# Moving half of one batch's exponentials from the SP queue to the ScalarE queue

## The chip, the cores and the metric

One Trainium2 chip; the kernel runs on one of its cores. The metric is the device time of one execution in microseconds (us). The engines are TensorE (PE: matrix products, with PEld for its weight loads), VectorE (DVE), ScalarE (ACT), GpSimd (POOL) and SyncE (SP). A transfer (DMA) is issued by an engine's queue, here SP's or ScalarE's (SPq and ACTq in the rows), and moved by DMA engines; each engine works through its own list of instructions in order, and they wait for each other with semaphores.

## What is computed

The reference is an attention of tokens against a small state, in both directions, and then a feed-forward network over both results. For each of 8 batches and 8 heads, with 512 tokens `x` and 32 state rows of 64 numbers:

```
scores  = scale * x @ state.T      a  = softmax(scores)     xread = a @ state
scores2 = scale * state @ x.T      a2 = softmax(scores2)    sread = a2 @ x
x   = concat(xread, sread) over tokens, heads side by side: 4352 rows of 512
h   = x @ w_in                                   (512 x 2048)
out = (h * clip(h + 3, 0, 6) / 6) @ w_out        (2048 x 512)
```

All of it is in float32.

## The kernel before

**Tiles and stages.** The work goes batch by batch. The feed-forward part of a batch is cut into 16 steps, one for each 128 columns of the hidden layer; step numbers run on over all batches, 0 to 143. In step n, `first(n)` forms the hidden values of 128 columns by 512 tokens in a PSUM bank `ps_h` (six matmuls, line 858). ScalarE makes `relu(h + 3)` from it (line 908), DVE takes the minimum with 6 and multiplies by h (line 910). The result `g` is split in two halves for PE: a cast on ScalarE (line 246, `g_hi`) and a subtraction on DVE (line 247, `g_lo`). Two steps later `second(n)` multiplies it with `w_out` into four PSUM accumulators `acc0` to `acc3` (twelve matmuls, also line 858, three for each accumulator). `ps_h` has two banks, so `first(n + 2)` waits until lines 908 and 910 of step n have read theirs. The product of the state with `w_in` (called W', lines 462, 246 and 247, in the banks `ps_s`) stands in for `xread @ w_in`, so `first` multiplies the weights `a` directly with W'.

**Batches 0 and 1 at the start.** The first two batches are interleaved with the loading of the weights: steps 0 to 3 are batch 0, 4 to 11 batch 1, 12 to 23 batch 0, 24 to 31 batch 1, then batches 2 to 7 follow. At the end of step 23 the accumulators of batch 0 are added to a partial result by four additions on DVE (line 947), one for each accumulator; `second(24)` may write an accumulator of the same name only after its addition has read it.

**The state's own attention.** For `sread`, the exponentials of `scores2` of batch b (line 718, on ScalarE) come in two groups g of 128 rows, one tile `tmp` each. To be used as PE weights they have to be turned. From batch 1 on, `weights_moved` does that in two parts: DVE transposes each 32 x 32 block in place (line 766 for batch 1, into the tile `blocks`), and then 16 transfers for each group set the blocks in their places in the tile `e2T` (line 773, 16 KB each, from SBUF to SBUF). `tokens_read(1)` then multiplies `e2T` with x (line 815, 64 matmuls, the first group's before the second's). It rides in one PE operation with the scores of batch 2: a transpose of batch 0's result (line 833), the 16 score matmuls (line 462), and line 815. In the plan this operation stands right behind `first(27)`. Batches 2 to 7 do the same with line 787 and one tile for both groups.

**What sets the order.** Every operation is given to a planner (`Plan`) with an engine (T, V, S or Q for PE, DVE, ScalarE and SP's transfers), a cost, a rank, and what it reads and writes. `Plan.order` steps through time: on each engine it looks at the operations that could start, takes those that could start within 0.3 us of the soonest, and of them the one of lowest rank, and by number where ranks are equal. Results count as visible 0.12 us after an operation of DVE or ScalarE and 0.25 us after one of PE. For SP's transfers it counts at most eight in flight:

```
        flying = [0.0] * 8
                    if e == "Q":
                        t = max(t, min(flying))
                    (c for c in can if c[0] <= soon + (0.8 if c[1] <= 0.0 else 0.3)),
                    key=lambda c: c[1:],
```

The order that comes out is written into the engines' lists; on the chip the engines follow it and the semaphores. The moves of batch 1 are told with rank `MOVED` = 22. In batches 0 and 1 the ranks of lines 908 and 910 and of the split (lines 246 and 247) are the step number; the additions of line 947 after step 23 have rank 25, and W' for the steps from 28 on has 25.4. In the program every transfer, of either queue, uses one of eight completion counters, taken in turn in the order of the plan, and waits before it is issued until the transfer that used that counter last has landed.

Other lines that are spoken of: 352 (cast of a piece of `w_out`), 962 (store of a batch's result), 382 (load of a batch's state), 969 (the last two stores, one from each queue).

Of the kernel before, what the change touches and what calls it, by code (L numbers as in the profile page):

```python
# [149 lines left out]
def tile_state_attention_then_hardswish_ffn(  # L150
# [8 lines left out]
    nc = tc.nc  # L159
# [65 lines left out]
    def V(cost, rank, do, reads=(), writes=(), after=()):  # L225
        return plan.add("V", cost, rank, do, reads, writes, after)

    def S_(cost, rank, do, reads=(), writes=(), after=()):
        return plan.add("S", cost, rank, do, reads, writes, after)

    def Q(rank, size, do, reads=(), writes=(), after=()):
        return plan.add("Q", 0.45, rank, do, reads, writes, after, size)

    def get(key, make):

        if key[:2] not in made:
            made[key[:2]] = make()
        return made[key[:2]]
# [277 lines left out]
    def tmp(key):  # L516

        return get(key, lambda: att.tile([P, S], F32, name="tmp", bufs=10))
# [218 lines left out]
    def e2T_key(b, g, *part):  # L737
        return ("tmp", ("e2T", b, g), *part) if b < TURNED else ("raw", ("e2T", b), *part)

    def e2T(b, g):  # L740

        return tmp(e2T_key(b, g)) if b < TURNED else made[e2T_key(b, g)][:, g]
# [16 lines left out]
    def weights_moved(b, rank, after=()):  # L759


        quarter = lambda k: slice(k * NS, (k + 1) * NS)
        if b < TURNED:
            for g in range(NG):
                blocks_key = ("tmp", ("blocks", b, g))
                V(0.62, rank, lambda g=g, key=blocks_key: nc.vector.transpose(
                    tmp(key), tmp(("tmp", ("e2", b, g)))), [("tmp", ("e2", b, g))], [blocks_key], after)
                for c in range(P // NS):
                    for q in range(NQ):
                        def move(c=c, q=q, g=g, key=blocks_key):  # L770
                            src = tmp(key)[quarter(q)].rearrange("p (j c n) -> p j c n", j=J, n=NS)
                            dst = e2T(b, g)[quarter(c)].rearrange("p (j q n) -> p j q n", j=J, n=NS)
                            nc.sync.dma_start(dst[:, :, q], src[:, :, c])  # L773
                        Q(rank, 16.384, move, [blocks_key], [e2T_key(b, g, c, q)])
            return
        blocks_key = ("raw", ("blocks", b))
        made_of = lambda key: get(key, lambda: stage.tile([P, NG, S], F32, name="raw"))
        for g in range(NG):
            V(0.62, rank, lambda g=g: nc.vector.transpose(
                made_of(blocks_key)[:, g], tmp(("tmp", ("e2", b, g)))),  # L780
                [("tmp", ("e2", b, g))], [(*blocks_key, g)])
        for c in range(P // NS):
            for q in range(NQ):
                def move(c=c, q=q):
                    src = made_of(blocks_key)[quarter(q)].rearrange("p g (j c n) -> p (g j) c n", j=J, n=NS)
                    dst = made_of(e2T_key(b, 0))[quarter(c)].rearrange("p g (j q n) -> p (g j) q n", j=J, n=NS)
                    nc.sync.dma_start(dst[:, :, q], src[:, :, c])  # L787
                Q(rank, 32.768, move, [(*blocks_key, g) for g in range(NG)], [e2T_key(b, 0, c, q)])
# [290 lines left out]
    def begin(b, s0, shift=0):  # L1079

        spots = [s0 + p + (shift if p else 0) for p in PLAN]
        rank, after = lambda k: spots[k] + 0.45, lambda k: [first_of[spots[k]]]
        at(spots[4] + 1, attention, b, rank, after)
        at(spots[7] + 1, lambda: weights_moved(b, rank(7)))
# [10 lines left out]
    for b, s0 in (0, 4), (1, 8):  # L1095

        def late(b=b, s0=s0):
# [4 lines left out]
            else:  # L1102
                load_x(1, AGAIN, (), True)
        at(LATE_TOLD[b], late)
    at(MOVED + 1, lambda: weights_moved(1, MOVED, [first_of[MOVED]]))
    fetch(2, 28, 20)
    for b in range(2, B):
# [20 lines left out]
    for n in range(len(steps)):  # L1128
        tell(n)
        b, i, _, _ = steps[n]  # L1130
        k, c = n // FPC, i // FPC
# [56 lines left out]
```

## Time and profile before

| what | value |
|---|---|
| time before, median of 3 runs | 659.69 us (659.68 to 659.81) |
| the profiled execution's own time | 660.08 us |
| its span, first to last instruction | 658.2 us |
| granted TensorE clock, mean | 0.999 |
| PE busy | 647.7 us (98%) |
| DVE busy | 420.4 us (64%) |
| ScalarE busy | 312.1 us (47%) |
| hardware-queue transfers from SP (q1) | 130704 packets, 45.37 MB |
| hardware-queue transfers from ScalarE (q10) | 144 packets, 0.26 MB |

The span is the time between the first and the last instruction in the profile; the device time has 1.88 us around it. Busy times are sums over an engine's instructions. Line numbers are those of the kernel before. In rows, "us" after a start is the time that a piece took, "xN" the number of instructions merged in it, and a bracket at the end is the idle time of the engine before it and what ended that.

### The profile page before, as it was taken

How to read it: one execution, taken by the hardware profiler on the slowest of the kernel's cores; microseconds unless marked ns; L12 is line 12 of the kernel's file. 1: busy time of each engine (PE TensorE's matmuls, PEld its weight loads, DVE VectorE, ACT ScalarE, POOL GpSimd, SP SyncE). 2: the span in 40 equal slices, each digit the busy share in tenths (PEclk: the TensorE clock that was granted, in tenths of full speed). 3: DMA queues.
4: the chain of work that ended last, by engine and by line, in shares of the span. 5: the costliest groups of instructions: out<-in, count | busy, mean ns of one | idle time of the engine just before them, and what ended most of it. 6: DMA issues, size and time to landing. Idle time of an engine off the chain costs nothing.

```text
span 658.2 us, 9905 instructions
## 1 busy us (share of the span) xinstructions
PE 647.7 (98%) x3934; PEld 502.1 (76%) x3934; DVE 420.4 (64%) x697; ACT 312.1 (47%) x522; POOL 1.0 (0%) x7
## 2 busy tenths in 40 slices
PE   7999999999999999999999999999999999999997
PEld 7447777777777877787877877787778788788896
DVE  4999999977756845954577356934595353443552
ACT  5889686643524543533444343534344343333542
POOL 0000000000000000000000000000000000000000
PEclk9999999999999999999999999999999999999999
DMA  8904742415163043323050504041131001000101
GB/s 266 318 1 160 196 150 106 98 27 138 19 144 58 15 75 85 66 32 65 17 116 14 83 1 121 13 64 32 64 66 28 5 1 65 0 1 1 64 1 33
DMA packets 130895, 46.26 MB, mean 70 GB/s; under 512 B 119201, under 2 KB 121249, under 8 KB 130721
## 3 DMA queue, kind: packets, MB, share of 16 engines
q1 hardware_dynamic: 130704, 45.37, 27.9%
q8 instruction: 31, 0.51, 0.3%
q10 hardware_dynamic: 144, 0.26, 0.1%
q14 instruction: 16, 0.12, 0.1%
HBM read 33.03 MB, written 8.91 MB: 64 GB/s over the span
## 4 chain that ended last, share of the span: by engine, by line
PE 89%; SPq 6%; DMA 2%; DVE 1%; issue 1%; ACT 0%; DVEq 0%; ACTq 0%
PE acc L858 51%; PE ps_h L858 27%; PE ps_s L462 4%; SPq L773 2%; PE acc L927 2%; SPq L787 2%; PE ps_h L462 2%; SPq L449 1%; PE ps_h L887 1%; PE ps_h L815 1%; DMA ot<-in_x_dram 1%; DMA tmp<-tmp 1%; PE ps_s L620 1%; DMA st_raw<-in_state_dram 0%; DMA raw<-in_x_dram 0%
## 5 line engine op out<-in xcount | busy, mean ns | idle before, releaser
L858 PE MATMUL acc<-w_out_hi,g_hi 128*128 128x512 f32 x528 | 208.9, 396 | 0.0
L858 PE MATMUL acc<-w_out_lo,g_hi 128*128 128x512 f32 x528 | 205.9, 390 | 0.0
L858 PE MATMUL acc<-w_out_hi,g_lo 128*128 128x512 f32 x528 | 205.7, 390 | 0.1
L908 ACT ACTIVATE g<-ps_h,three 128x512 f32<-128x512 f32 (+1 forms) x144 | 95.7, 664 | 211.3 <-PE ps_h L858 210.4
L910 DVE SCALAR_TENSOR_TENSOR g<-g,ps_h 128x512 f32<-128x512 f32 (+1 forms) x144 | 94.6, 657 | 134.6 <-ACT g L908 133.3
L858 PEld LDWEIGHTS acc<-w_out_hi,g_hi 128*128 128x128 f32 x528 | 99.1, 188 | 34.0 <-issue 11.3
L246 ACT CAST g_hi<-g 128x512 fp32r<-128x512 f32 (+1 forms) x140 | 83.2, 596 | 81.6 <-DVE g L910 81.1
L247 DVE TENSOR_TENSOR g_lo<-g,g_hi 128x512 fp32r<-128x512 f32 (+1 forms) x140 | 92.0, 658 | 46.0 <-ACT g_hi L246 44.2
L858 PEld LDWEIGHTS acc<-w_out_hi,g_lo 128*128 128x128 f32 x528 | 99.1, 188 | 21.5 <-DVE g_lo L247 0.6
L858 PEld LDWEIGHTS acc<-w_out_lo,g_hi 128*128 128x128 f32 x528 | 99.2, 188 | 19.1
L858 PE MATMUL ps_h<-aT_hi,wp_hi 128*128 128x512 f32 (+1 forms) x248 | 90.6, 365 | 0.0
L858 PE MATMUL ps_h<-aT_hi,wp_lo 128*128 128x512 f32 (+1 forms) x248 | 89.8, 362 | 0.0
L858 PE MATMUL ps_h<-aT_lo,wp_hi 128*128 128x512 f32 (+1 forms) x248 | 89.7, 362 | 0.0
L858 PEld LDWEIGHTS ps_h<-aT_hi,wp_hi 128*128 128x128 f32 x248 | 46.8, 189 | 8.5 <-DVE g L910 0.5
L858 PEld LDWEIGHTS ps_h<-aT_lo,wp_hi 128*128 128x128 f32 x248 | 46.8, 189 | 8.2 <-issue 0.5
L858 PEld LDWEIGHTS ps_h<-aT_hi,wp_lo 128*128 128x128 f32 x248 | 46.8, 189 | 7.2
L858 PE MATMUL ps_h<-aT_hi,wp 128*128 128x512 f32 x128 | 44.6, 389 | 0.0
L858 PEld LDWEIGHTS ps_h<-aT_hi,wp 128*128 128x128 f32 x128 | 24.0, 188 | 5.0
L858 PE MATMUL ps_h<-aT_lo,wp 128*128 128x512 f32 x64 | 24.9, 389 | 0.0
L462 PE MATMUL ps_s<-w_in,stT 64*32 64x512 f32 (+1 forms) x368 | 22.9, 555 | 0.0
L546 DVE STREAM_TRANSPOSE tmp<-raw 128x512 f32<-128x512 f32 x24 | 16.4, 698 | 7.1 <-DMA raw<-in_x_dram 7.1
L247 DVE TENSOR_TENSOR wp_lo<-ps_s,wp_hi 128x512 fp32r<-128x512 f32 (+1 forms) x34 | 19.7, 618 | 0.0
(123 smaller groups left out, 504.7 us busy)
## 6 DMA issues: line engine op xcount, KB each, us to landing
out_dram<-ot SPq DMA_DIRECT2D x8, 1024.0 KB, 4.4
early<-in_moe_w_in_dram SPq DMA_DIRECT2D x7, 1024.0 KB, 6.7
xb<-in_x_dram SPq DMA_DIRECT2D x28, 256.0 KB, 4.3
raw<-in_x_dram SPq DMA_DIRECT2D x96, 64.0 KB, 2.1
early<-in_moe_w_out_dram SPq DMA_DIRECT2D x4, 1024.0 KB, 5.8
raw<-in_moe_w_out_dram SPq DMA_DIRECT2D x7, 512.0 KB, 5.3
raw<-raw SPq DMA_DIRECT2D x96, 32.0 KB, 1.9
early<-in_moe_w_in_dram SPq DMA_DIRECT2D x2, 512.0 KB, 5.9
```

The costliest lines, as they stand in the source:

```text
L246: S_(cost, rank, lambda: nc.scalar.copy(hi(), src()), reads, [writes[0]])
L247: V(cost, rank, lambda: nc.vector.tensor_tensor(lo(), src(), hi().bitcast(F32), op=ALU.subtract), [*reads, writes[0]], [writes[1]])
L449: nc.sync.dma_start(t[rows, i].rearrange("t (a c) -> t a c", c=NS), x[b, 4 * g + 2 * i + u, :, k * NS : (k + 1) * NS].rearrange("(a t) c - ...
L462: nc.tensor.matmul(out[u][cols, :], made["stT", b][rows, cols], moving(q)[rows], start=True, stop=True,)
L546: V(0.7, rank, lambda q=q, key=key: nc.vector.transpose(xT(b, q), made[key][:, q % 2]), [(*key, q % 2, u, k) for u in range(2) for k in ra ...
L620: nc.tensor.matmul(out[:, j, q], xT(b, q)[:, js], apart[:, q], start=True, stop=True,)
L773: nc.sync.dma_start(dst[:, :, q], src[:, :, c])
L787: nc.sync.dma_start(dst[:, :, q], src[:, :, c])
L858: nc.tensor.matmul(ps, l, r, start=start and k == 0, stop=stop and k == n - 1)
L908: S_(cost + 0.05, rank, lambda: nc.scalar.activation(g(), bank(ps)[:, :width], AF.Relu, bias=three), [ps], [g_key])
L910: V(cost, rank, lambda: nc.vector.scalar_tensor_tensor(g(), g(), 6.0, bank(ps)[:, :width], op0=ALU.min, op1=ALU.mult), [ps], [g_key])
L927: nc.tensor.matmul(bank(acc), made["g_hi", n][:, js], plain_out[i][1](), start=opens, stop=closes)
```

## The change

In `weights_moved`, for batch 1 alone, the 16 transfers of the second group (g = 1) are issued by ScalarE's queue, and are told to the planner as ScalarE operations of 0.5 us with the rank 22 + 2.6 = 24.6. The first group's 16 stay with SP, as transfers of rank 22.

```diff
                 for c in range(P // NS):
                     for q in range(NQ):
-                        def move(c=c, q=q, g=g, key=blocks_key):
+                        def move(c=c, q=q, g=g, key=blocks_key, queue=(nc.sync, nc.scalar)[g]):
                             src = tmp(key)[quarter(q)].rearrange("p (j c n) -> p j c n", j=J, n=NS)
                             dst = e2T(b, g)[quarter(c)].rearrange("p (j q n) -> p j q n", j=J, n=NS)
-                            nc.sync.dma_start(dst[:, :, q], src[:, :, c])
-                        Q(rank, 16.384, move, [blocks_key], [e2T_key(b, g, c, q)])
+                            queue.dma_start(dst[:, :, q], src[:, :, c])
+                        if g:
+                            S_(0.5, rank + 2.6, move, [blocks_key], [e2T_key(b, g, c, q)])
+                        else:
+                            Q(rank, 16.384, move, [blocks_key], [e2T_key(b, g, c, q)])
```

## Rows read from the trace of the kernel before

**Rows 1.** The page's first part: busy time of each engine over the span.
```profile
PE 647.7 (98%) x3934; PEld 502.1 (76%) x3934; DVE 420.4 (64%) x697; ACT 312.1 (47%) x522; POOL 1.0 (0%) x7
```

**Rows 2.** Timeline of SP's queue, 129 to 151 us: start, time taken, line.
```profile
129.25 21.59 SPq L773 DMA_DIRECT2D tmp<-tmp  x32
150.94 0.54 SPq L962 DMA_DIRECT2D out_dram<-ot  x1
```

**Rows 3.** Line 773 by itself: durations in ns (minimum, median, maximum).
```profile
L773 SPq DMA_DIRECT2D tmp<-tmp x32: 586/599/988, 129.3 to 150.2; - x32
```

**Rows 4.** Timeline of PE at `tokens_read` of batch 1, from line 833 on.
```profile
149.80 0.27 PE L833 MATMUL ps_h<-ident,tmp 128*128 128x128 f32 x1
...
152.21 0.61 PE L815 MATMUL ps_h<-xb,tmp 128*32 128x64 f32 x26 [0.37 <-DMA tmp<-tmp]
152.74 0.50 PE L858 MATMUL acc<-w_out_hi,g_hi 128*128 128x512 f32 x1
```

**Rows 5.** Timeline of PE at the same operation for batch 2.
```profile
206.56 0.27 PE L833 MATMUL ps_h<-ident,tmp 128*128 128x128 f32 x1
...
208.81 0.50 PE L858 MATMUL acc<-w_out_hi,g_hi 128*128 128x512 f32 x1
```

**Rows 6.** Line 969, the last two stores: durations in ns and starts.
```profile
L969 SPq DMA_DIRECT2D out_dram<-ot x1: 615/615/615, 653.6 to 653.6; - x1
L969 ACTq DMA_DIRECT2D out_dram<-ot x1: 659/659/659, 654.2 to 654.2; - x1
```

**Rows 7.** Timeline of DVE, 129 to 149 us.
```profile
129.81 0.71 DVE L766 STREAM_TRANSPOSE tmp<-tmp 128x512 f32<-128x512 f32 x1
...
141.35 0.69 DVE L910 SCALAR_TENSOR_TENSOR g<-g,ps_h 128x512 f32<-128x512 f32 x1
...
143.09 0.68 DVE L247 TENSOR_TENSOR g_lo<-g,g_hi 128x512 fp32r<-128x512 f32 x1
143.69 1.88 DVE L947 SCALAR_TENSOR_TENSOR ot<-acc,ot 128x512 f32<-128x512 f32 x3
145.49 1.28 DVE L247 TENSOR_TENSOR wp_lo<-ps_s,wp_hi 128x512 fp32r<-128x512 f32 x2
...
148.07 0.69 DVE L247 TENSOR_TENSOR g_lo<-g,g_hi 128x512 fp32r<-128x512 f32 x1 [0.69 <-ACT g_hi L246]
```

**Rows 8.** Chain of waits, 129 to 139 us: SP's fourth, seventh, eleventh issue; a landing.
```profile
131.79 0.60 SPq L773
...
133.71 0.60 SPq L773
...
136.30 0.60 SPq L773
...
138.23 1.85 DMA tmp<-tmp
```

**Rows 9.** Line 908 from 132.4 to 132.6 us: ScalarE's queue reads step 23's semaphore.
```profile
L908 ACTq EVENT_SEMAPHORE  x1: 17/17/17, 132.4 to 132.4; - x1
```

**Rows 10.** Timeline of ScalarE, 133 to 148 us: steps 23 to 26.
```profile
133.55 0.68 ACT L908 ACTIVATE g<-ps_h,three 128x512 f32<-128x512 f32 x1
135.60 0.67 ACT L352 CAST w_out_hi<-raw 128x512 fp32r<-128x512 f32 x1 [1.38 <-DVE raw L327]
...
136.84 0.69 ACT L908 ACTIVATE g<-ps_h,three 128x512 f32<-128x512 f32 x1
138.82 0.62 ACT L246 CAST g_hi<-g 128x512 fp32r<-128x512 f32 x1 [1.30 <-DVE g L910]
140.63 0.69 ACT L908 ACTIVATE g<-ps_h,three 128x512 f32<-128x512 f32 x1 [1.19 <-PE ps_h L858]
...
142.13 0.62 ACT L246 CAST g_hi<-g 128x512 fp32r<-128x512 f32 x1
...
147.42 0.62 ACT L246 CAST g_hi<-g 128x512 fp32r<-128x512 f32 x1 [0.76 <-DVE g L910]
```

**Rows 11.** Timeline of PE: step 24's first matmul into the fourth accumulator.
```profile
147.75 0.39 PE L858 MATMUL acc<-w_out_hi,g_hi 128*128 128x512 f32 x1
```

## Prediction

> **What bounds the kernel now.** The page's first part comes first: PE is busy 647.7 us, 98% of the span, and the other engines far less [rows 1]. So only what lets PE wait, or ends a wait, counts. The change touches one place, the 32 transfers of line 773, so I read the timelines of SP, PE, ScalarE and DVE around them. SP issues all 32 in one stretch of 21.59 us from 129.25, one every 0.645 us [rows 2], each 599 ns long [rows 3]. Their reader is `tokens_read` of batch 1, the matmuls of line 815, and PE shows a wait of 0.37 us for the last of them, up to 152.21 [rows 4]. That understates it: from line 833 to the next line 858 the stretch takes 152.74 - 149.80 = 2.94 us here, and the same work in batch 2, whose transfers are in time, takes 208.81 - 206.56 = 2.25 [rows 4, 5]. So late transfers cost **0.69 us**, and no other wait of PE hangs on them. That is the whole prize: 0.1% of the time.
>
> **What is removed.** SP loses 16 issues, 16 x 0.645 = 10.3 us, and is done at about 139.6. Behind them on SP stand the store of batch 0 [rows 2] and then the load of batch 3's state; they go earlier, and no engine waits for either: nothing gained. If the second group lands before 151.0, the 0.69 us go, and the next thing late there is nothing that PE shows.
>
> **What is added.** ScalarE gets 16 issues. Its one issue in this trace, the last store, takes 659 ns against 615 for SP's store of the same size [rows 6]. Scaled, 599 x 659 / 615 = 0.64, with SP's gap of 0.045 it is 0.69 us each, 11.0 in all. Bounds: 0.645 (as SP) and 0.70 (the store's own, with the gap). I take 0.69, from the same engine.
>
> **Where they stand in ScalarE's order.** The planner decides this by rank. The moves have 24.6, steps up to 24 rank lower and go first, step 25 and its W' halves (25.4) rank higher and go last. Worked by hand from the planner's costs (0.5 a move, about 0.65 an activation or copy, its 0.3 us of choice): one move before the scaling of the last weight piece, three behind step 23's activation, one behind its cast, two behind step 24's activation, and the remaining **nine behind step 24's cast, ahead of step 25's activation**. On DVE the same working puts step 25's line 910 between the second and the third of the four line 947 additions, which empty the accumulators of batch 0, and its line 247 between the third and the fourth. Before, both stood ahead of the last three additions [rows 7].
>
> **When they run.** In the program each transfer takes one of eight completion counters in turn, over both queues, and is issued when the transfer eight places before it in the plan has landed (the planner's `flying` has eight entries too). Interleaved with SP's sixteen, the second move waits for SP's fourth, the fourth for its seventh, the fifth for its eleventh. SP's times are 131.79, 133.71 and 136.30, and one lands 1.85 us later [rows 8]: 133.64, 135.56, 138.15. ScalarE's queue works ahead of its engine: step 23's semaphore was read at 132.4, a microsecond before that activation ran [rows 9, 10]. So an issue can lie beside the activation before it, but not beside a wait. Step by step:
> - First move at 130.55, when the second transposition is done (129.81 + 0.71, [rows 7]); three from 133.65 to 136.25. The cast of line 352, at 135.60 before [rows 10], slips 0.65, and step 23's cast with it: both have slack.
> - Fifth move at 138.15, so step 24's activation is at 138.87 instead of 136.84 [rows 10]. Two moves; its cast at 140.35.
> - Nine moves from 140.3: 9 x 0.69 = 6.2. **Step 25's activation starts at 146.5 instead of 140.63** [rows 10].
> - Behind it, by start to start: 0.72 to DVE's 910, 0.78 to the cast (140.63, 141.35, 142.13), 0.65 to the 247 (147.42, 148.07), 0.60 to the last 947 (143.09, 143.69), 0.69 until it is done [rows 7, 10]: 3.44, or 149.95.
> - PE's step 24 writes the fourth accumulator at 147.75 [rows 11]. It may not until the last 947 has read it: a stall of **2.2 us**. The third is free earlier, by the same sum without the cast, the 247 and one 947, and its wait lies inside this.
> - Behind the last 947 DVE has the two W' subtractions and step 26's 910, 1.28 + 0.69 [rows 7]: 151.9, and with that the bank is free that line 833 writes; PE gets there at 149.80 + 2.2 = 152.0. No second stall. The last move lands at 147.7, in time.
>
> Sum: + 2.2 - 0.69 = **+1.5 us**. The profiled execution is 660.08, its span 658.2 and 1.88 around it; it would be 661.6. It lies 0.39 above the median of 659.69, and on that I put 661.2. About 0.2%, 1.3 us, is what a measurement of this kernel tells from no change, so 661.2 is just beyond it.
>
> The nearest rows for two queues issuing at once are the last two stores: SP's runs from 653.6 for 0.615, ScalarE's starts at 654.2 [rows 6]. They hardly overlap, so the trace leaves open whether one queue's issue holds up the other's. Bounds: nothing, and a full issue (0.645) per move while SP still issues; I take nothing, since the later store is longer by only 0.044.
>
> **Rivals.**
> *ScalarE is early enough* (not slower). If the counters never bind and a move costs 0.645 as on SP, the fifth move goes at 136.25, step 24's activation and cast stay at 136.84 and 138.82, and nine moves end at 144.7. The point that decides is 147.75 - 3.44 = 144.3 for step 25's activation with no stall, and 145.0 with a stall equal to the prize. At 144.7 the stall is 0.4: 659.69 + 0.4 - 0.69 = 659.4; without any stall 659.0. For it: ScalarE is busy under half of its time [rows 1]. Against it: landings of 1.85 us are in the trace, and ScalarE's own issue is the longer. Chance 0.25.
> *The two queues take turns.* If each of the first four moves pushes SP's stream by 0.6, SP's eleventh lands 2.4 us later, step 24's activation and all behind it slip by 2.4, and the stall is 4.6: 659.69 + 4.6 - 0.69 = 663.6; half of it gives 662.4. For it: both queues are busy from 130.5 to 139.6. Against: the overlap is over before the nine. Chance 0.2. [...]
> *The order is not as worked out*, and the moves stand elsewhere: with the nine behind step 25's activation there is no stall, the last lands after 152 and the old wait stays, 659.7 give or take 1.5. One choice of the planner (910 before the third 947) rests on 0.07 us. Chance 0.08.
>
> **How the numbers follow.** The forecast has 0.47, from 660.6 (0.645 a move: 0.4 less over nine, 0.2 less ahead of them) to 661.8 (0.70 a move and landings of 2 us), so 0.28 of it is slower and 0.19 same. First rival: 0.24 same, 0.01 faster. Second: 0.2 slower. Third: 0.04 same, 0.02 each side. Together 0.50 slower, 0.47 same, 0.03 faster. The range runs from 659.2, in the first rival, to 663.0, in the second; it leaves out its far end and parts of the third. The forecast's own range is 660.6 to 661.8.
>
> **What would show it.** In the timeline of ScalarE: sixteen issues of line 773 from 130.5 on, nine in a row, then line 908 near 146.5. In PE's: a wait of about 2 us before a line 858 accumulator matmul near 147.5 to 150, put down to DVE's 947; line 815 with no wait on a transfer. Wrong: a 908 before 145.0, SP's issues longer than 0.65 while ScalarE issues, or the stall at another matmul.

## The result, and the profile after

The changed kernel takes 662.46 us (median of 6 runs, 661.30 to 663.75) against 659.68 of the kernel before (6 runs beside it, 659.44 to 659.81): ratio 1.0044, 95% interval 1.0034 to 1.0053. It is **slower by 2.8 us**; the forecast was 661.2, with a range to 663.0. The profiled execution took 661.67, its span 659.8. In the changed kernel all lines behind the diff stand three higher: 858 is 861, 908 is 911, 910 is 913, 947 is 950, 815 is 818, 833 is 836.

The page's first part, as [rows 1], and the first group of its fifth part (busy time, mean ns of one, idle time before it and what ended it):

```profile
PE 647.8 (98%) x3934; PEld 501.8 (76%) x3934; DVE 420.5 (64%) x697; ACT 312.3 (47%) x522; POOL 1.0 (0%) x7
...
L861 PE MATMUL acc<-w_out_hi,g_hi 128*128 128x512 f32 x528 | 209.0, 396 | 2.1 <-DVE ot L950 2.1
```

No engine does more work than before. What is new is idle time of PE, 2.1 us, that DVE's additions end. ScalarE's timeline shows where it begins (compare [rows 10]):

```profile
129.90 0.71 ACTq L773 DMA_DIRECT2D tmp<-tmp  x1
...
131.84 0.60 ACTq L773 DMA_DIRECT2D tmp<-tmp  x1
...
132.79 1.34 ACTq L773 DMA_DIRECT2D tmp<-tmp  x2
...
135.40 0.59 ACTq L773 DMA_DIRECT2D tmp<-tmp  x1
...
136.12 2.06 ACTq L773 DMA_DIRECT2D tmp<-tmp  x2
138.22 0.62 ACT L246 CAST g_hi<-g 128x512 fp32r<-128x512 f32 x1 [1.43 <-DVE g L913]
138.93 7.13 ACTq L773 DMA_DIRECT2D tmp<-tmp  x9
146.16 0.69 ACT L911 ACTIVATE g<-ps_h,three 128x512 f32<-128x512 f32 x1 [7.32 <-DMA tmp<-tmp]
```

Seven of the sixteen moves lie between other work, and nine stand in a row between step 24's cast and step 25's activation. They take 7.13 us, and the activation that started at 140.63 before starts at 146.16. On DVE, whose order is fixed, everything behind step 25's line 913 waits for it (compare [rows 7]):

```profile
141.83 1.38 DVE L950 SCALAR_TENSOR_TENSOR ot<-acc,ot 128x512 f32<-128x512 f32 x2 [1.04 <-PE acc L861]
146.88 0.69 DVE L913 SCALAR_TENSOR_TENSOR g<-g,ps_h 128x512 f32<-128x512 f32 x1 [3.67 <-ACT g L911]
147.49 0.68 DVE L950 SCALAR_TENSOR_TENSOR ot<-acc,ot 128x512 f32<-128x512 f32 x1
148.25 0.69 DVE L247 TENSOR_TENSOR g_lo<-g,g_hi 128x512 fp32r<-128x512 f32 x1
148.86 0.68 DVE L950 SCALAR_TENSOR_TENSOR ot<-acc,ot 128x512 f32<-128x512 f32 x1
```

Two of the four additions are done early; the third and the fourth have nothing to do with step 25, yet stand behind its 913 and its 247. And PE waits for just these two (its timeline, compare [rows 4, 11]):

```profile
145.06 0.39 PE L861 MATMUL acc<-w_out_hi,g_hi 128*128 128x512 f32 x1
...
148.23 0.50 PE L861 MATMUL acc<-w_out_hi,g_hi 128*128 128x512 f32 x1 [1.65 <-DVE ot L950]
...
149.60 0.50 PE L861 MATMUL acc<-w_out_hi,g_hi 128*128 128x512 f32 x1 [0.41 <-DVE ot L950]
...
151.78 0.27 PE L836 MATMUL ps_h<-ident,tmp 128*128 128x128 f32 x1
...
153.00 1.27 PE L818 MATMUL ps_h<-xb,tmp 128*32 128x64 f32 x64
154.20 0.50 PE L861 MATMUL acc<-w_out_hi,g_hi 128*128 128x512 f32 x1
```

Line 818 runs through without a wait, so the transfers are in time now: from 836 to the next 861 it takes 154.20 - 151.78 = 2.42 us instead of 2.94, and 0.52 is won. Ahead of that, from step 24's first matmul (145.06; it was at 145.71 before) to line 836, it takes 6.72 us instead of 4.09, and 2.63 is lost. Net: **+2.11 us**.

To compare executions I use one stretch below: from step 24's first accumulator matmul to the first one behind line 815 or 818. It takes 152.74 - 145.71 = 7.03 us before and 154.20 - 145.06 = 9.14 after. The instant at which it begins differs by over a microsecond from execution to execution, also where the program up to there is the same (145.06 in this profile, 146.53 in that of the longer wait below). It was 0.65 earlier in this profile than in that of before, which is why the two profiled executions differ by only 1.59.

### The profile page after: what moved, and what is told of

It reads as the page before. It is cut to its first block, busy times and chain, and to the rows that moved or that the text cites. A ratio compares the mean times of both kernels' runs of the same rounds, so it can differ in the third digit from the quotient of the medians.

```text
span 659.8 us, 9900 instructions
## 1 busy us (share of the span) xinstructions
PE 647.8 (98%) x3934; PEld 501.8 (76%) x3934; DVE 420.5 (64%) x697; ACT 312.3 (47%) x522; POOL 1.0 (0%) x7
## 4 chain that ended last, share of the span: by engine, by line
PE 94%; DMA 2%; SPq 2%; DVE 1%; ACT 0%; issue 0%; ACTq 0%
PE acc L861 53%; PE ps_h L861 28%; PE ps_s L462 4%; PE acc L930 2%; PE ps_h L462 2%; SPq L773 1%; DMA st_raw<-in_state_dram 1%; PE ps_h L818 1%; PE ps_h L890 1%; DMA tmp<-tmp 1%; PE ps_s L620 1%; PE acc L555 0%; DVE g L913 0%; ACT g L911 0%; DVE g_lo L247 0%
```

## The experiments

**The changed kernel again**, for the spread of its runs.

> The changed kernel once more. Its six executions so far lie in two groups, 661.3 to 661.7 and 663.2 to 663.8 us. Theory of the counters: moves of ScalarE wait for loads of batch 3's state that took the same completion counters, and these loads land at varying times; then the executions spread again over 661.3 to 663.8, and a profile of a late one shows step 25's activation (line 911) some 2 us later than 146.2, with gaps between ScalarE's last issues. Rival (the spread comes from the start of the kernel or from the end): line 911 of step 25 keeps its distance from step 24's cast, about 8 us, whatever the time.

Measured: 662.82 us (5 runs, 662.60 to 664.05) against 659.74 before, ratio 1.0051 (1.0038 to 1.0064). The theory of the counters was wrong: in the profiled execution, of 663.20, step 25's activation came at 146.63, 7.86 us behind step 24's cast against 7.94 in the first profile, which is the rival's sign. Nor do the five fall into two groups. But this profile shows something that the first did not. First its timeline of PE, then busy times by stretch with the granted clock of PE as a share of full speed (columns: from and to, length, PE, PEld, DVE, ACT, POOL with numbers of instructions, PEclk, DMA share, GB/s):

```profile
145.15 0.39 PE L861 MATMUL acc<-w_out_hi,g_hi 128*128 128x512 f32 x1
...
148.69 0.50 PE L861 MATMUL acc<-w_out_hi,g_hi 128*128 128x512 f32 x1 [2.02 <-DVE ot L950]
...
150.07 0.79 PE L861 MATMUL acc<-w_out_hi,g_hi 128*128 128x512 f32 x1 [0.40 <-DVE ot L950]
150.66 0.63 PE L861 MATMUL acc<-w_out_lo,g_hi 128*128 128x512 f32 x1
...
153.65 0.27 PE L836 MATMUL ps_h<-ident,tmp 128*128 128x128 f32 x1
...
156.04 0.50 PE L861 MATMUL acc<-w_out_hi,g_hi 128*128 128x512 f32 x1
```
```profile
147.00:149.00 2.00, 0.31 (x1) 0.30 (x2) 1.57 (x3) 1.72 (x4) 0.00 (x0) 1.00 0.05 8
149.00:151.00 2.00, 1.60 (x5) 1.02 (x4) 2.00 (x4) 0.76 (x2) 0.00 (x0) 0.68 0.12 49
151.00:153.00 2.00, 2.00 (x6) 1.52 (x5) 1.32 (x3) 0.62 (x1) 0.00 (x0) 0.50 0.99 410
153.00:155.00 2.00, 2.00 (x28) 0.78 (x31) 0.56 (x2) 0.69 (x1) 0.00 (x0) 0.97 0.16 66
```

The granted clock, 1.00 up to the wait, fell to 0.50 behind it, with matmuls of 0.63 us in place of 0.39, and stayed there for about 3 us. From the fourth accumulator to line 836 it takes 3.58 us; in the first profile, which shows 1.00 throughout, it took 2.18. So this execution paid 1.4 us more for the same place: its stretch is 10.89 us. The nine moves take as long in both (7.09 and 7.13 us); they start 0.4 us later here, counted from the beginning of the stretch, and the wait is longer by that.

**All moves later by rank** (behind step 26 instead of behind step 24).

```diff
-                            S_(0.5, rank + 2.6, move, [blocks_key], [e2T_key(b, g, c, q)])
+                            S_(0.5, rank + 5.0, move, [blocks_key], [e2T_key(b, g, c, q)])
```

> The same change with one number different: the moves get rank 27 instead of 24.6, so in the plan step 25's activation, its casts and step 26's activation go ahead of the moves that are left. Theory of the order (the nine moves in a row hold up step 25's activation, and by it DVE's additions and PE): no wait of PE on line 950, the last move lands before or near PE's line 818, and the time is 659.0 to 659.7. Rival (the issues of the two queues hold each other up, or 16 issues on ScalarE cost PE time wherever they stand): 661 or more.

Measured: 658.71 us (11 runs, 658.45 to 659.02), ratio 0.9984 (0.9976 to 0.9993). ScalarE's timeline:

```profile
138.35 1.91 ACTq L773 DMA_DIRECT2D tmp<-tmp  x3
140.36 0.69 ACT L911 ACTIVATE g<-ps_h,three 128x512 f32<-128x512 f32 x1 [1.50 <-DMA tmp<-tmp]
140.38 0.59 ACTq L773 DMA_DIRECT2D tmp<-tmp  x1
...
142.44 3.04 ACTq L773 DMA_DIRECT2D tmp<-tmp  x3
```

The same sixteen issues on the same queue, but with three ahead of step 25's activation instead of nine. That activation is on time, and on DVE the order of before is back, with step 25's 247 ahead of the last three additions:

```profile
142.52 0.68 DVE L247 TENSOR_TENSOR g_lo<-g,g_hi 128x512 fp32r<-128x512 f32 x1
143.12 1.88 DVE L950 SCALAR_TENSOR_TENSOR ot<-acc,ot 128x512 f32<-128x512 f32 x3
```

PE has no wait in the stretch, and the stretch is 6.49 us against 7.03: the prize of the change, 0.54, without its price. The transfers are no less in time: line 818 waits for none. This kernel beats both. Its median is 1.0 us under that of before; the half of it that the stretch doesn't show is not located.

**Half of the moves back on SP** (8 of the group's 16 stay on ScalarE, at the changed kernel's rank).

```diff
-... queue=(nc.sync, nc.scalar)[g]):
+... queue=(nc.sync, nc.scalar)[g and c < 2]):
...
-                        if g:
+                        if g and c < 2:
```

> Only half of the second group (c = 0 and 1, eight moves) goes by ScalarE; the other eight stay with SP behind the first group. Rank 24.6 as in the change. Of the nine moves behind step 24's cast one is left. Theory of the order: no stall at the accumulators; SP is done at about 145 and the last lands near 146.8, before line 818 at 151.0, so the prize of 0.5 to 0.7 us comes in: 659.0 to 659.3. Rival (two queues at once are slow in themselves): over 660.

Measured: 658.90 us (11 runs, 658.38 to 659.61), ratio 0.9989 (0.9980 to 0.9998). Step 25's activation is at 140.09, the stretch 6.51 us without a wait. Eight moves find room between ScalarE's other work, and DVE's order is that of before here too; the eight more, all behind step 24's cast, did the harm.

**The load of batch 3's state told later.** In the changed program the four transfers of that load (line 382, on SP, which is free early) had fallen between ScalarE's seventh and tenth move in the turn of the eight completion counters. So ScalarE's moves drew the counters of SP's last issues, and of the loads themselves. The chain of waits shows it: SP's last move goes out and lands, and only then does ScalarE's tenth begin:

```profile
139.16 1.90 DMA tmp<-tmp
141.06 0.02 issue
141.08 0.59 ACTq L773
```

The edit tells that load two steps later, so that all moves come ahead of it:

```diff
-        at(s0 + 1, lambda: load_state(b, s0, [first_of[s0]]))
+        at(s0 + (3 if b == 3 else 1), lambda: load_state(b, s0, [first_of[s0 + (2 if b == 3 else 0)]]))
```

> The changed kernel, but the load of batch 3's state is planned two steps later (behind first(28)), so that none of its four transfers stands between ScalarE's moves in the turn of the completion counters. Theory of the counters: the spread goes, all executions lie within 0.5 us of each other, at 661.0 to 661.8, since the stall at the accumulators of about 2 us stays. Rival (the spread has another cause): executions at 663.2 to 663.8 are still among them.

Measured: 660.31 us (11 runs, 659.52 to 662.01), ratio 1.0010 (1.0001 to 1.0020), 2.5 us under the changed kernel beside it. ScalarE and PE:

```profile
138.29 5.82 ACTq L773 DMA_DIRECT2D tmp<-tmp  x9
144.21 0.69 ACT L911 ACTIVATE g<-ps_h,three 128x512 f32<-128x512 f32 x1 [5.32 <-DMA tmp<-tmp]
```
```profile
147.66 0.50 PE L861 MATMUL acc<-w_out_hi,g_hi 128*128 128x512 f32 x1 [0.27 <-DVE ot L950]
```

What was expected did not come: the spread is still 2.5 us, and the time is lower than forecast, because the stall all but went. DVE's order is the changed one here (two additions, 913, 950, 247, 950), so this run changes ScalarE's lateness without that order. The nine moves now take 0.65 us each and begin earlier; step 25's activation is 1.95 us earlier and PE's wait is 0.27 instead of 1.65 and 0.41. The stretch is 7.05, as long as before: prize and price cancel. The profiled execution was the quickest of the eleven; what makes the others up to 2.5 us longer no profile shows. Their mean granted clock doesn't tell: it was 0.999 in the longest.

The **same edit on the kernel before** is the control.

> The kernel before, with the load of batch 3's state told two steps later, as in the run that took 2.5 us off the changed kernel. My theory: there it only took these loads out of the turn of the completion counters between ScalarE's moves; the kernel before has no moves on ScalarE, so nothing changes: 659.7 give or take 0.5. Rival: the later load helps by itself (it frees DMA engines or a buffer), 658 or less.

Measured: 659.60 us against 659.88, ratio 0.9997 (0.9988 to 1.0006), its wait for transfers the same 0.37 us as in [rows 4]. The later load helps nothing by itself; it only keeps the loads out of the moves' turn.

**PE kept busy where it waits.**

```diff
                 w = [w_out_of(h, i, 1)[:, 0, :] for h in ("hi", "lo")]
+                for _ in range(7 if n == 24 and acc[0] == "acc1" else 0):
+                    nc.tensor.matmul(bank(acc), hi[:, js], w[0], start=True, stop=True)
```

> Changed kernel, with the first matmul of step 24's second accumulator done seven times over ahead of its product (7 x 0.227 = 1.6 us of matmuls whose result the product overwrites). They stand just where PE otherwise waits 1.65 to 2.02 us for DVE's second-but-one addition, so nothing on DVE or ScalarE moves. My theory: ScalarE's lateness fixes when the third and fourth accumulators come free (148.2 and 149.6), and the runs of 663 us are those in which PE's granted clock fell to 0.50 behind its idle time. With PE busy there the wait before the third accumulator shrinks to under 0.4 us, the granted clock stays at 1.00 from 147 to 155, line 836 follows the fourth accumulator after 2.2 us (not 3.6), and the time is 661.3 to 661.9 in every run, none above 662.5: about 1.1 us under the changed kernel's 662.8. Rival: the runs of 663 us come from ScalarE or the counters being later in them; then the spread stays and the median is 662.5 or more. Second rival: the repeats simply add their 1.6 us, 664.4.

Measured: 662.01 us (5 runs, 661.37 to 663.11). The profiled execution took 662.89, in PE's timeline (936 are the repeats; 952 is the addition, line 950 elsewhere):

```profile
147.01 1.75 PE L936 MATMUL acc<-w_out_hi,g_hi 128*128 128x512 f32 x7
...
149.91 0.50 PE L861 MATMUL acc<-w_out_hi,g_hi 128*128 128x512 f32 x1 [0.48 <-DVE ot L952]
```

The seven repeats' 1.6 us are nearly free: the stretch is 9.57 us (146.33 to 155.90) against 9.14, and that 0.43 is ScalarE's, whose step 25 activation came 147.85 - 146.33 = 1.52 us behind step 24's first matmul instead of 146.16 - 145.06 = 1.10. PE had nothing better to do there. The granted clock is 1.00 in all windows from 140 to 157. One profile doesn't prove that the repeats held it there, since one of the changed kernel's four shows no fall either. And "none above 662.5" was wrong: this execution is long because its stretch began at 146.33, 1.27 us later than in the first profile, and the median is 0.8 lower, not 1.1. That lateness is older than the stretch: SP's first move starts at 130.01 here, at 128.39 in the first profile. Over the first 40 us the granted clock is 0.96 here, against 1.00 in the first profile and in that of before; how much of the lateness that makes no run shows. The profile of the longer wait below began late too, at 146.53. The spread has two sources, then: what lies ahead of the stretch, whose beginning differs without the change too (145.71 before, 145.15 with the state load later), and the clock behind PE's wait.

**PE's wait made longer.**

```diff
-        S_(cost + 0.05, rank, lambda: nc.scalar.activation(
-            g(), bank(ps)[:, :width], AF.Relu, bias=three), [ps], [g_key])
+        S_(cost + 0.05, rank, lambda: [nc.scalar.activation(
+            g(), bank(ps)[:, :width], AF.Relu, bias=three) for _ in range(4 if n == 25 else 1)], [ps], [g_key])
```

> Changed kernel, with step 25's activation done four times over on ScalarE (three more at 0.58 us, 1.74 us), so that PE's wait before the third accumulator grows from 1.65 to 2.02 us to 3.4 to 3.8. My theory: idle time of PE there is paid in full, and where it lasts about 2 us or more the granted clock falls behind it; then it falls here in every execution: PEclk under 0.75 in the 2 us behind the wait, matmuls 0.63 us long instead of 0.39, and from the end of the wait to line 836 5.0 us or more instead of 3.55 (after the changed kernel's profile: 148.23 to 151.78). Time 662.8 + 1.74 = 664.5, and more by up to 1 where the changed kernel's own median holds executions without the fall: 664.5 to 665.6. Rival: the fall in one execution was chance and has nothing to do with the wait; then PEclk stays at 1.00 and the time is 663.4 (661.7 + 1.74). Second rival: a wait there is partly hidden by slack behind it; then under 663.

Measured: 665.78 us (4 runs, 664.85 to 667.49). The wait and the clock behind it:

```profile
151.92 0.50 PE L861 MATMUL acc<-w_out_hi,g_hi 128*128 128x512 f32 x1 [3.86 <-DVE ot L950]
```
```profile
149.00:151.00 2.00, 0.00 (x0) 0.00 (x0) 0.43 (x1) 1.94 (x4) 0.00 (x0) 1.00 0.00 0
151.00:153.00 2.00, 0.97 (x3) 0.48 (x3) 1.92 (x4) 1.71 (x4) 0.00 (x0) 0.97 0.00 0
153.00:155.00 2.00, 1.71 (x4) 1.42 (x5) 2.00 (x4) 0.00 (x0) 0.00 (x0) 0.50 0.47 197
```

The clock fell again, and from the wait's end to line 836 it took 156.84 - 151.92 = 4.92 us, against 3.55 without the fall. The stretch is 12.72 us, 1.83 over the 10.89 of the changed kernel's execution with the wait of 2.02. The three activations more cost ScalarE 2.15 us, not the 1.74 expected (from 147.70 to its next work at 150.44 is 2.74, where one activation took 0.59), and step 25's first came 0.31 earlier in the stretch (1.17 us behind its beginning against 1.48): 1.84 in all. Lateness there is paid in full. The median is just above what was expected, and this execution is also one of the two that began late.

**Two more profiled executions of the changed kernel.**

> The changed kernel once more, one profile. My theory: from step 24's first matmul to the first accumulator matmul behind line 818 it takes 9.1 us where PEclk holds 1.00 (as 145.06 to 154.20) and 10.9 where it falls behind the wait (as 145.15 to 156.04), against 7.03 before; the execution's time less the instant at which that stretch ends is 507.2 give or take 0.4 in either case. Rival: the time is lost or won elsewhere too, and that remainder is off by 1 us or more.

> The changed kernel once more, one profile; as the look before it: a stretch of 9.1 us with PEclk at 1.00 or of 10.9 with a fall, and a remainder of 507.2 give or take 0.4. With both, the rule that a wait near 2 us lets the clock fall has two more cases: the wait with the fall is the longer one.

Measured: 662.94 and 663.00 us. Both show the fall, at waits a little under the 2 us that was expected to be needed; here the first one's wait and its clock:

```profile
148.47 0.50 PE L861 MATMUL acc<-w_out_hi,g_hi 128*128 128x512 f32 x1 [1.85 <-DVE ot L950]
```
```profile
149.00:151.00 2.00, 1.60 (x5) 0.97 (x5) 2.00 (x5) 0.54 (x1) 0.00 (x0) 0.72 0.16 66
151.00:153.00 2.00, 2.00 (x6) 1.51 (x5) 1.28 (x2) 0.62 (x1) 0.00 (x0) 0.50 1.07 442
```

Their stretches are 10.90 and 10.87 us, their waits 1.85 and 1.81. All profiles side by side (us; the clock is the granted one within the stretch, and the last column is the execution's time less the instant at which the stretch ends):

| kernel | time | stretch begins | its length | longest wait of PE in it | clock | rest |
|---|---|---|---|---|---|---|
| before | 660.08 | 145.71 | 7.03 | 0.37 | 1.00 | 507.3 |
| changed, first | 661.67 | 145.06 | 9.14 | 1.65 | 1.00 | 507.5 |
| changed, again | 663.20 | 145.15 | 10.89 | 2.02 | falls | 507.2 |
| changed, two more | 662.94, 663.00 | 145.10, 145.16 | 10.90, 10.87 | 1.85, 1.81 | falls | 506.9, 507.0 |
| moves later by rank | 658.52 | 145.15 | 6.49 | none | 1.00 | 506.9 |
| half back on SP | 658.50 | 145.17 | 6.51 | none | 1.00 | 506.8 |
| state load later | 659.52 | 145.19 | 7.05 | 0.27 | 1.00 | 507.3 |
| before, state load later | 659.13 | 145.15 | 7.00 | 0.37 | 1.00 | 507.0 |
| PE kept busy | 662.89 | 146.33 | 9.57 | 0.48 | 1.00 | 507.0 |
| additions first (next) | 662.11 | 145.44 | 9.24 | 1.23 | 1.00 | 507.4 |
| wait made longer | 666.60 | 146.53 | 12.72 | 3.86 | falls | 507.4 |

The rest is the same within 0.7 us. All that the change does to the time of these executions happens in this stretch.

**The additions put first on DVE.** The store of batch 0 is held in its place, so that the transfers keep their turns.

```diff
-            rank = n + LAG
+            rank = n + LAG - (0.1 if more and n == 23 else 0)
...
-              [(*ot_key, j) for j in range(nt)])
+              [(*ot_key, j) for j in range(nt)] + ([("g_hi", 25)] if n == 23 else []))
```

> Changed kernel, with the four additions that empty batch 0's accumulators ranked 24.9 instead of 25, so that all four stand ahead of step 25's line 913 on DVE (and W' is cast ahead of step 25's cast on ScalarE); transfers and ScalarE's moves stay where they are. My theory: PE's wait before the accumulators is only the order on DVE; it goes, the wait moves to where step 26's result frees the bank that line 836 writes, and because ScalarE is as late as before most of the time stays lost: line 836 near 151.0 with a wait of 1 to 2 us put down to DVE's 913 or ScalarE's 911, 661.8 us, or 660.9 where the clock holds. Rival: the addition order is the whole cost; then no wait of over 0.4 us is left and the time is 659.2.

Measured: 661.40 us (11 runs, 660.66 to 662.13), ratio 1.0024 (1.0014 to 1.0033). DVE does all four additions in a row now, and PE waits elsewhere:

```profile
142.21 2.76 DVE L950 SCALAR_TENSOR_TENSOR ot<-acc,ot 128x512 f32<-128x512 f32 x4 [0.54 <-PE acc L861]
```
```profile
149.55 0.50 PE L861 MATMUL ps_h<-aT_hi,wp_hi 128*128 128x512 f32 x1 [1.23 <-DVE g L913]
...
152.23 0.33 PE L836 MATMUL ps_h<-ident,tmp 128*128 128x128 f32 x1 [1.02 <-DVE g L913]
```

The wait for the additions is gone, and two others stand in its place, for the bank that step 25 has to empty (which I had not expected) and then for step 26's (which I had). The stretch is 9.24 us, no shorter than the 9.14 of the changed kernel with its clock up. But ScalarE was still later here: the nine moves took 8.39 us, and step 25's activation came at 148.09, 2.65 us behind the beginning of the stretch instead of 1.10. From that activation to line 836 it takes 152.23 - 148.09 = 4.14 us instead of 151.78 - 146.16 = 5.62. So the order on DVE decides where PE waits, and at the same lateness of ScalarE the changed kernel's order costs about 1.5 us more (an estimate from these two profiles; where W' stands on ScalarE moved as well); that PE waits at all comes from ScalarE.

## Why the prediction was right, and by how much it was off

**The number** lies in the stated range, but above the forecast's own 660.6 to 661.8. The range reached up to 663.0 only for the sake of the rival of the two queues, which did not happen; that the median of 662.46 is inside is luck. The direction, and the part of the time that the mechanism explains, are not.

**The mechanism** was right from end to end: nine moves between step 24's cast and step 25's activation, the order 910, 947, 247, 947 on DVE, a wait before the third and the fourth accumulator, line 815 without a wait, no second stall. The runs back its parts: with the moves elsewhere there is only a gain (658.71), with ScalarE's row of moves earlier and DVE's order kept the stall all but goes (660.31), and with ScalarE made later still there is more loss (665.78).

**The prize** of 0.69 was 0.52 to 0.54. Batch 2's stretch of 2.25 us was the wrong yardstick; where line 818 waits for nothing in this place, with the clock at 1.00, it takes 2.39 to 2.45. The difference is in the 64 matmuls themselves: 1.03 us in batch 2 (207.78 to 208.81, before), 1.20 here (153.00 to 154.20).

**ScalarE's lateness** came out nearly right by luck, from errors that cancel. An issue takes 612 ns and comes every 0.65 us where nothing stops it, the low end of the bounds (0.69 was taken; nine in 5.82 us with the loads out of the way). But nine took 7.13, since the loads of batch 3's state took turns of the counters; I had costed their going earlier at "nothing gained", and did not ask what it would take. The earlier moves, on the other hand, went before their forecast: in the built program the fourth move, not the second, has the counter of SP's fourth, and the seventh, not the fifth, that of its eleventh. So the fifth went at 135.40, where 138.15 was forecast. Put on the same footing (this execution's stretch began 0.65 earlier), step 25's activation was forecast for 145.85 and came at 146.16.

**The stall** of 2.2 us measured 149.60 - 147.10 = 2.50 at the fourth accumulator (147.10 is [rows 11] less 0.65): 0.31 for the later activation, less 0.06 for the tail behind it, which took 149.54 - 146.16 = 3.38 instead of 3.44, plus 0.06 from the addition's end to the matmul. Another 0.13 goes by up to line 836, since the first matmul behind a wait takes 0.50 us where it took 0.39. So +2.63 - 0.52 = +2.11 where the sum had +1.5.

**The term that was missing** is the clock. The sum took PE's idle time as the whole price of a wait. In four of the five profiles of this place with a wait of 1.65 us or more (three of the changed kernel, and the longer wait), the granted clock fell to 0.50 behind it, and that costs 1.4 to 1.6 us more: from the end of the wait to the end of the stretch it takes 7.33 to 7.53 us with the fall and 5.97 without. The changed kernel's profiled executions with the fall took 662.94 to 663.20, the one without 661.67. For the others there is only the mean granted clock of the whole execution, which doesn't say where it fell: it is 0.997 or less in ten of the thirteen executions of the changed kernel (661.68 to 664.05) and 1.000 in three (661.30, 661.67, 662.60); of the 55 of the kernel before that ran beside the experiments six have 0.997 or less. That fits a fall in most executions of the changed kernel, without showing it for each.

**The rivals.** ScalarE early enough was a matter of the state's load: with it out of the turn, step 25's activation lies 0.98 us ahead of step 24's first matmul, which is 144.7 in the forecast's frame, this rival's own figure, and that profiled execution took 659.5 for its 659.4; its median is still 660.31. The two queues taking turns would have pushed SP by 0.6 us for each move; it did not happen. While ScalarE issues two moves, from 136.12 and from 137.59, of 0.59 us each, SP's issues in the chain of waits read

```profile
136.39 0.60 SPq L773
...
137.03 0.64 SPq L773
...
137.72 0.60 SPq L773
...
138.36 0.75 SPq L773
```

and its sixteen took 11.37 us, 0.71 each, against 0.675 as the mean of [rows 2] (the prediction's 0.645 is the usual distance of two issues, not that mean). Of the prediction's signs of being wrong this one showed in part: two of SP's issues beside ScalarE's took 0.80 and 0.75 us (from 133.53 and 138.36). But two others, with none of ScalarE's beside them, took 0.76 and 0.68 (from 128.39 and 134.38), and issues of the two queues overlap, SP's from 137.72 with ScalarE's from 137.59 for most of its length, and both are of the usual length, 0.60 and 0.59; by the two means the price is a few hundredths of a microsecond each. That one queue's issue holds up the other's for a whole issue, as this rival took it, is not what the trace shows; a much shorter hold these rows can't exclude. The time that this rival gave, 662.4 to 663.6, was reached in another way. The order was as worked out.

## What to carry to other kernels

Moving sixteen issues to a half-idle engine (47% busy) was free here only where they lay between its other work: with nine in a row ahead of step 25's activation the kernel took 662.46 us, with three 658.71. So count how many stand in one row ahead of an instruction that another engine's order hangs on, and split or rank them so that the row is short. What stands behind that instruction in the other engine's list matters as much: work that doesn't need it is better put ahead of it. The queue that was relieved ran its next transfers sooner (the state's load from 139.80 us, from 151.5 before), and as the program's completion counters go round over both queues these took turns ahead of work that mattered more: the nine moves took 7.13 us, and 5.82 with the load later. The price of a new wait on PE was its idle time plus, in the four profiles where the clock fell to 0.50 behind it, the matmuls that then ran longer: 1.4 to 1.6 us.

## What was not expected of the hardware

In four profiles the granted clock behind PE's wait (2.02, 1.85, 1.81 and 3.86 us) went from 1.00 to 0.50; the fall begins not with the wait but 1.0 to 1.9 us after its end (an estimate from the granted clock of the 2 us in which it begins, 0.68, 0.72, 0.84 and 0.97, with 1.00 ahead of it and 0.50 behind; in the first of them the third accumulator at 148.69 is still 0.50 us long, the fourth at 150.07 already 0.79), and it lasts some 3 us while PE is busy. In the profile with a wait of 1.65 it stayed at 1.00, as it did with PE kept busy up to a wait of 0.48, and with the additions first, where two waits of 1.23 and 1.02 follow each other. What exactly decides it these runs don't settle.

Issues on ScalarE's queue are hardly dearer than SP's: 612 ns in the median against 604 in the same execution of the changed kernel, with both queues at work, and 599 for SP alone [rows 3].
